# Placing the early raw inputs, the first weights and the v step of a fused attention, dense and expert kernel

## The chip, the cores and the metric

One core of a Trainium2 chip runs the whole kernel. The metric is the device time of one execution in microseconds; less is better. Runs of one kernel are given with their median.

## The reference, cut to what matters

```python
# q, k, v: (4, 8, 576, 64) float32; w_in (512, 2048), w_out (2048, 512) arrive as float64
scores = scale * (q @ k.T)                       # per batch and head
kth = np.partition(scores, -32, axis=-1)[..., -32:-31]
scores = np.where(scores >= kth, scores, -1e9)   # the 32 largest of each row stay
attn = softmax(scores)
x = (attn @ v)                                   # -> 2304 tokens of 512
x = softplus(x @ w_in) @ w_out                   # dense layer, hidden size 2048
e = argmax(x @ w_gate); g = softmax(x @ w_gate)[e]
out = g * (relu(x @ w1[e]) @ w2[e])              # one of 8 experts for each token
```

## The kernel before, in words

`part_one` does attention and the dense layer, `part_two` the experts. Two heads of one batch make a pair; batch 0 has pairs 0 to 3 in the list `pairs`, called the first to the fourth pair here (m = 0 to 3), and 16 loads of each of q, k and v are made in all. A pair is prepared once for its visits: q, k and v are loaded into tiles of 128 partitions by 576 float32 (`qn`, `kn`, `vn` from the pool `raw`, which has one buffer of each, RB = 1), their magnitudes are summed on ACT (`magnitudes`, line 338), and each is split into a half of 16 bits and the rest (lines 370 and 371 for k and q, 383 and 384 for v; the subtraction runs on DVE for the first pair and on POOL for the others). The halves of k are transposed by a DMA into `kt` (line 373), those of q by two DMAs into `q1` (line 376); two plain copies make `q2`, the same with its halves of partitions exchanged (lines 377 and 378). The halves of v are copied into `v16` by six DMAs (lines 388 to 390). `prep_split` does all this for the first four pairs, `prep_step` in three steps for all later ones. All these DMAs are issued on one queue, SP's, which works in order.

Attention runs over groups of two score tiles of 128 by 576. Each pair has two groups in the first sweep over batch 0, so the first pair belongs to groups 0 and 1, the second to 2 and 3, the third to 4 and 5, the fourth to 6 and 7. `emit_scores` makes a group's scores on PE (line 456, results `sa` and `sb`; a score needs q1, q2 and kt), `emit_softmax` finds the 32nd largest score on DVE (lines 496 to 522) and makes the masked exponents on ACT and POOL (lines 530 to 542), and a DMA transposes them (line 544). Three groups later (LAG = 3) `emit_av` multiplies them with v (line 559).

The weights of the dense layer come as float64 and are decoded in 32 chunks of 128 by 512: `decode` loads a chunk (line 238), and ACT, DVE and POOL build float32 from its words (lines 247 to 253); for w_in ACT and POOL then split it (lines 258 to 260). The list `dec_q` holds four chunks of w_in, then rows 0 to 3 of w_out, four of w_in, rows 4 to 7, and so on. `decode_some(2)` takes two of them ahead of the first group, and four more are emitted with each group (DECR = 4). The decoded w_out, `w_out_s`, is one tile of 16 rows (KF) of 512 float32 for each partition; its row f is first read by the second product of the dense layer (line 686).

When the tiles of a unit (two tiles of 128 tokens, in most) are complete, `moe_step` runs the dense layer on it, 16 steps of line 646 (x @ w_in) and line 686, and `route` then writes its rows and its places in `table`, which `clear_table` has filled beforehand. The first unit is complete after group 7, the second after the next sweep.

The order on each engine's queue and on SP's is set when the kernel is built, by a planner that runs a timeline with its own costs: of what is ready it takes what has the highest priority. Priority is the place in the program, moved forward by the offset of `tc.high_priority` (A_PREP = 150, AHEAD = 100). `tc.issue_after(x)` puts what is traced in its block behind x on x's queue.

## Time and profile before

| what | value |
| --- | --- |
| median of 3 runs | 1064.67 us (1059.51, 1064.67, 1066.27) |
| the profiled execution | 1059.72 us |
| its span in the trace | 1058.0 us |
| mean granted clock of TensorE | 0.936 of full speed |
| DMA | 156.97 MB, mean 148 GB/s |

The span is the time from the first to the last instruction that the trace shows; the profiled execution's own time is 1.72 us longer. In the rows below PE is TensorE, PEld its weight loads, DVE VectorE, ACT ScalarE, POOL GpSimd and SP the engine that issues DMAs (SPq is its queue). A time in brackets is how long the engine stood idle before the instruction, with what ended the wait. "x4" counts instructions that were merged into a row.

### The profile page before, as it was taken

To read this page: it belongs to the slowest core of one execution; us is meant where nothing else is said; L and a number is where in the kernel's file an instruction comes from. 1 tells how busy PE (TensorE), PEld (TensorE's weight loads), DVE (VectorE), ACT (ScalarE), POOL (GpSimd) and SP (SyncE) were. 2 spreads that over 40 slices of the span, in tenths; PEclk is the share of its full clock that TensorE was granted. 3 is DMA by queue.
4 is the path that set the end of the run, shared out by engine and by line. 5 is a ranking of instruction groups with operands and counts; after the bars stand their busy time and mean duration, and the time that the engine had idled before them with its cause. 6 is when DMAs were issued, how large, how long until landed. Compare 5 with 4: busy or idle time off the path is not lost.

```text
span 1058.0 us, 22206 instructions
## 1 busy us (share of the span) xinstructions
PE 885.0 (84%) x7146; PEld 655.0 (62%) x7146; DVE 849.3 (80%) x3021; ACT 801.2 (76%) x1866; POOL 604.0 (57%) x631
## 2 busy tenths in 40 slices
PE   1124359774998989998999999999999999999994
PEld 0013236443675656675666666676787989999993
DVE  4779999998997968996989999955356987777773
ACT  5878898988888979987998888863678555555552
POOL 3888898998767768876778777652001022111111
PEclk9986559876999989998999999999999999999998
DMA  7897799788799987669978855464301667666650
GB/s 188 193 205 189 180 192 193 179 168 172 114 131 164 138 152 129 117 80 150 152 131 120 99 90 95 72 86 131 102 12 31 170 220 243 242 212 230 237 202 23
DMA packets 295859, 156.97 MB, mean 148 GB/s; under 512 B 257524, under 2 KB 257652, under 8 KB 295732
## 3 DMA queue, kind: packets, MB, share of 16 engines
q1 hardware_dynamic: 292116, 145.73, 67.1%
q0 software_dynamic: 3616, 9.72, 2.6%
q8 instruction: 58, 0.95, 0.4%
q14 instruction: 69, 0.57, 0.2%
HBM read 77.89 MB, written 11.11 MB: 84 GB/s over the span
## 4 chain that ended last, share of the span: by engine, by line
PE 47%; DVE 13%; DMA 12%; ACT 9%; POOL 8%; issue 6%; SPq 4%; POOLq 0%; ACTq 0%; DVEq 0%
PE h L646 11%; PE h L996 9%; PE y L686 8%; PE y L1009 8%; PE y L683 3%; DVE mx L522 3%; DVE wk L518 3%; DMA xT<-xh 3%; POOL e L531 2%; POOL p L542 2%; DMA w<-in_moe_w_in_dram 2%; PE sb L456 2%; PE m L559 1%; ACT e L532 1%; PE sa L456 1%
## 5 line engine op out<-in xcount | busy, mean ns | idle before, releaser
L646 PE MATMUL h<-xT,w_in_s 128*128 128x256 f16 (+1 forms) x1920 | 228.7, 269 | 22.9 <-ACT sa L660 14.4
L686 PE MATMUL y<-w_out_s,g 128*128 128x512 f32 x480 | 229.0, 601 | 1.3 <-ACT g L661 1.2
L646 PEld LDWEIGHTS <-w_in_s 128*128 128x128 f16 x1920 | 174.9, 101 | 82.7 <-issue 52.7
L531 POOL TENSOR_TENSOR e<-s,e 128x576 f32<-128x576 f32 x144 | 204.0, 1432 | 17.7 <-ACT e L530 10.4
L522 DVE MAX8 mx<-wk 128x8 f32<-128x128 f32 (+2 forms) x432 | 200.9, 503 | 0.1
L542 POOL TENSOR_TENSOR p<-e,p 128x512 f16<-128x512 f32 x144 | 167.8, 1165 | 0.0
L456 PEld LDWEIGHTS <-q 128*128 128x128 f16 (+1 forms) x640 | 55.8, 108 | 175.4 <-issue 125.8
L518 DVE MATCH_REPLACE8 wk<-mx,wk 128x128 f32<-128x128 f32 (+1 forms) x432 | 145.1, 343 | 0.1
L686 PEld LDWEIGHTS y<-w_out_s,g 128*128 128x128 f32 x480 | 82.7, 192 | 64.0 <-issue 58.1
L976 POOL DMA_INDIRECT out_dram<-ot,idx x19 | 19.5, 1028 | 176.1 <-DVE ot L975 173.4
L532 ACT ACTIVATE e<-e,bias 128x576 f32<-128x576 f32 x144 | 110.4, 768 | 12.7 <-POOL e L531 12.2
L996 PEld LDWEIGHTS h<-xT,wf 128*128 128x128 f32 x864 | 111.8, 191 | 5.4 <-ACT wf L957 0.2
L996 PE MATMUL h<-xT,wf 128*128 128x256 f32 x864 | 113.9, 283 | 0.0
L456 PE MATMUL sa<-kt,q 128*128 128x256 f16 (+1 forms) x320 | 54.0, 302 | 71.0 <-DMA kt<-st 23.4
L1009 PE MATMUL y<-wf,hT 128*128 128x512 f32 x432 | 112.8, 398 | 0.0
L456 PE MATMUL sb<-kt,q 128*128 128x320 f16 (+1 forms) x320 | 62.7, 338 | 53.6 <-ACT s L502 53.5
L530 ACT ACTIVATE e<-s,kths 128x576 f32<-128x576 f32 x144 | 104.9, 767 | 0.8
L559 PEld LDWEIGHTS <-pT 128*128 128x128 f16 (+1 forms) x1440 | 86.8, 106 | 22.9 <-issue 19.8
L559 PE MATMUL m<-v,pT 128*128 128x65 f16 (+1 forms) x1440 | 93.9, 201 | 7.2 <-DVE xtail L586 4.3
L540 ACT ACTIVATE p<-e 128x576 f16<-128x576 f32 x144 | 97.4, 678 | 0.7
L541 POOL TENSOR_TENSOR p<-e,p 128x64 f16<-128x64 f32 x144 | 46.1, 320 | 70.4 <-ACT p L540 65.9
L1009 PEld LDWEIGHTS y<-wf,hT 128*128 128x128 f32 x432 | 76.7, 189 | 13.0
(235 smaller groups left out, 1791.1 us busy)
## 6 DMA issues: line engine op xcount, KB each, us to landing
w1r<-in_moe_w_dram SPq DMA_DIRECT2D x20, 1024.0 KB, 6.3
w2r<-in_moe_w_dram SPq DMA_DIRECT2D x20, 1024.0 KB, 7.8
w<-in_moe_w_in_dram SPq DMA_DIRECT2D x16, 512.0 KB, 4.0
w<-in_moe_w_out_dram SPq DMA_DIRECT2D x16, 512.0 KB, 4.0
rows<-xr SPq DMA_DIRECT2D x37, 128.2 KB, 3.1
qn<-in_q_dram SPq DMA_DIRECT2D x16, 288.0 KB, 4.1
kn<-in_k_dram SPq DMA_DIRECT2D x16, 288.0 KB, 6.1
vn<-in_v_dram SPq DMA_DIRECT2D x16, 288.0 KB, 3.5
```

Of the source, the lines that this page charges most:

```text
L456: last_qk[0] = nc.tensor.matmul(ps[p0:p1], lhsT=qs[:, h, r0:r1, :].rearrange("p r d -> p (r d)"), rhs=kt[:, k0:k1, cs], start=first, stop= ...
L518: nc.vector.match_replace(out=to, in_to_replace=mx[:, i, 8 * j:8 * j + 8], in_values=src[i], imm_value=NEG)
L522: nc.vector.max(out=mx[:, i, 8 * j + 8:8 * j + 16], in_=src[i])
L530: nc.scalar.activation(e[i], s[i], AF.Relu, bias=kths[:, 2 * gi + i], scale=-K_UP)
L531: nc.gpsimd.tensor_tensor(out=e[i], in0=s[i], in1=e[i], op=ALU.subtract)
L532: nc.scalar.activation(e[i], e[i], AF.Exp, bias=bt[:, i], scale=SCORE)
L542: nc.gpsimd.tensor_tensor(out=p16[:, S + D:], in0=e[i][:, 0:S - D], in1=p16[:, 0:S - D], op=ALU.subtract)
L559: nc.tensor.matmul(o[:, h, 0:D + 1], lhsT=pT(r), rhs=v16[:, h, c, 0:D + 1], start=r == 0, stop=r == R - 1)
L646: nc.tensor.matmul(hps[:, :n], lhsT=w_in_s[:, c, j, p, o:o + 128], rhs=xT[:, 0:len(u.tiles), r, c, :], start=m == 0, stop=m == 3 * KD - 1)
L686: nc.tensor.matmul(u.y[i], lhsT=g[:, cs], rhs=w_out_s[:, f, :], start=f == 0, stop=f == KF - 1)
L996: nc.tensor.matmul(h, lhsT=w1f[:, a, c, :], rhs=xT[:, b, c, :], start=n == 0, stop=n == 3 * KD - 1)
L1009: nc.tensor.matmul(y[i], lhsT=hT[g][:, a, i * 128:i * 128 + 128], rhs=w2f[:, b, :], start=g == 0 and n == 0, stop=g == KF2 - 1 and n == 2)
```

## The change

- The second pair's raw q, k and v are loaded into rows 12 to 15 of `w_out_s`, the third pair's into rows 8 to 11 (`ROOM`), which no weight has been written to yet. The second pair's loads are issued right behind the first's; the third's and the fourth's (which stays in `raw`) behind the first pair's last q transpose; the fifth's after the fourth is split.
- The halves of the second pair (k, q and v) lie in rows 4 to 7 of `w_out_s` (`STROOM`) instead of the pools `stg` and `row`.
- The v step of the first four pairs becomes a function, `prep_v`, that is traced at offset 20 (`A_V`) instead of 150; the first pair's magnitudes go with it.
- The first two weight chunks are traced at offset 150, behind the first pair's last q transpose.
- The fill of `table` is traced after them; its source lies in the last 146 columns of row 15 of `w_out_s`, no longer in a pool of its own.

Nothing of what is computed changes. The second pass that the kernel holds for inputs outside its bounds (`flags is None`) keeps the old loads. The diff:

```diff
@@ -48,6 +48,10 @@
 KVB = 4
 SWEEPS = [((0, 1), (8, 2, 3))] * 3 + [((0, 1), (8, 2), (3,))]
 UNITS = [[(b,2*i),(b,2*i+1)] for b in range(3) for i in range(2)]+[[(0,'tail0')],[(3,0),(3,1)],[(3,2),(1,'tail1')],[(3,3)]]
+ROOM = {1: 12, 2: 8}
+STROOM = 4
+V_NOW = 0
+A_V = 20
 XB = 1
 FLB = 4
 RB = 1
@@ -122,12 +126,6 @@
     table = dram.tile([E * NT + SLOT, 1], I32, name="table")
     rows = dram.tile([NT + 1, ROWW], F32, name="rows")
 
-    def clear_table():
-        with tc.tile_pool(name="fill", bufs=1) as p:
-            fill = p.tile([128, (E * NT + SLOT) // 128], I32, name="fill")
-            nc.gpsimd.iota(fill, pattern=[[0, (E * NT + SLOT) // 128]], base=TRASH, channel_multiplier=0)
-            nc.sync.dma_start(table.rearrange("(p a) o -> p (a o)", p=128), fill)
-
     zrow = const.tile([27, 19], F32, name="zrow")
     nc.vector.memset(zrow, 0.0)
     nc.sync.dma_start(rows[TRASH:TRASH + 1, :].rearrange("o (p a) -> (o p) a", a=19), zrow)
@@ -176,7 +174,6 @@
 
     def run(halves):
         nc.vector.memset(done, 0.0)
-        clear_table()
         with ExitStack() as p:
             late = part_one(tc, p, q, k, v, w_in, w_out, const, ident, before, ones, iota_e, reg_e, wg, ids,
                             ohcum, done, early, table, rows, flags if halves else None, sums, w_sums, e_sums, kths)
@@ -279,6 +276,11 @@
         nc.vector.tensor_scalar(bb, pb[:, 0:n], 1e-30, None, op0=ALU.max)
         return bb
 
+    def clear_table():
+        fill = w_out_s[:, KF - 1, DM - (E * NT + SLOT) // 128:].bitcast(I32)
+        nc.gpsimd.iota(fill, pattern=[[0, (E * NT + SLOT) // 128]], base=TRASH, channel_multiplier=0)
+        nc.sync.dma_start(table.rearrange("(p a) o -> p (a o)", p=128), fill)
+
     w_inv = wp.tile([128, DFF // C], F32, name="w_inv")
 
     def split_w_in(j):
@@ -313,27 +315,31 @@
                 f(*a)
 
 
-    pair = {}
+    pair, raws, last_t, last_l = {}, {}, {}, [None]
     v_up = wp.tile([128, B], F32, name="v_up")
     nc.vector.memset(v_up, 3.0e38)
 
     def load(m, i):
         b, hp = pairs[m]
-        t = raw.tile([128, R * D], F32, name="qkv"[i] + "n")
-        nc.sync.dma_start(t, (q, k, v)[i][b, 2 * hp:2 * hp + 2].rearrange("h (p r) d -> (h p) (r d)", r=R))
+        if flags is not None and m in ROOM:
+            a = ROOM[m] * DM + i * R * D
+            t = w_out_s.rearrange("p k c -> p (k c)")[:, a:a + R * D]
+        else:
+            t = raw.tile([128, R * D], F32, name="qkv"[i] + "n")
+        last_l[0] = nc.sync.dma_start(t, (q, k, v)[i][b, 2 * hp:2 * hp + 2].rearrange("h (p r) d -> (h p) (r d)", r=R))
         pair[m][0][i] = t
 
     def prep_load(m):
         src = [None] * 3
         bd = sm.tile([128, 3], F32, name="bd") if flags is None else sums[:, m]
-        pair[m] = (src, bd)
+        pair[m] = raws[m] = (src, bd)
         for i in range(3):
             load(m, i)
         if flags is None:
             magnitudes(m, stg.tile([128, R * D], F16, name="st"))
 
     def magnitudes(m, junk):
-        src, bd = pair[m]
+        src, bd = raws[m]
         for i, t in enumerate(src):
             nc.scalar.activation(junk, t, AF.Abs, accum_out=bd[:, i:i + 1])
 
@@ -353,6 +359,20 @@
             nc.scalar.activation(src[i], src[i], AF.Copy, scale=sc[:, i:i + 1])
         pair[m] = (*src, sc)
 
+    def staging(m, i):
+        cols = 2 * D + 2 if i == 2 else 2 * D
+        if flags is not None and m == 1:
+            a = STROOM * DM * 2 + i * R * 2 * D
+            st = w_out_s.rearrange("p k c -> p (k c)").bitcast(F16)[:, a:a + R * cols]
+            st = st.rearrange("p (r c) -> p r c", c=cols)
+        elif i == 2:
+            st = stg.tile([128, R, cols], F16, name="vs")
+        elif i and m < ST0:
+            st = row.tile([128, R, 2, D], F16, name="p16", bufs=PB if flags is not None else 2)
+        else:
+            st = stg.tile([128, R, 2, D], F16, name="st")
+        return st if i == 2 or len(st.shape) == 4 else st.rearrange("p r (s d) -> p r s d", d=D)
+
     def prep_split(m):
         qn, kn, vn, sc = pair[m] if flags is None else (*pair[m][0], None)
         sub = nc.vector if m < DVS else nc.gpsimd
@@ -363,22 +383,26 @@
             magnitudes(m, q2[:, 0].rearrange("p r d -> p (r d)"))
         for i, xs in enumerate((kn, qn)):
             xv = xs.rearrange("p (r d) -> p r d", d=D)
-            if i and m < ST0:
-                st = row.tile([128, R, 2, D], F16, name="p16", bufs=PB if flags is not None else 2)
-            else:
-                st = stg.tile([128, R, 2, D], F16, name="st")
+            st = staging(m, i)
             nc.scalar.activation(st[:, :, 0, :], xv, AF.Copy)
             sub.tensor_tensor(out=st[:, :, 1, :], in0=xv, in1=st[:, :, 0, :], op=ALU.subtract)
             if i == 0:
                 nc.sync.dma_start_transpose(out=kt, in_=st.rearrange("p r s d -> p (r s d)"))
             else:
                 for h in range(2):
-                    nc.sync.dma_start_transpose(out=q1[:, h], in_=st[64 * h:64 * h + 64].rearrange("p r s d -> p (r s d)"))
+                    last_t[m] = nc.sync.dma_start_transpose(
+                        out=q1[:, h], in_=st[64 * h:64 * h + 64].rearrange("p r s d -> p (r s d)"))
         nc.sync.dma_start(q2[0:64], q1[64:128])
         nc.sync.dma_start(q2[64:128], q1[0:64])
-
+        pair[m] = q1, q2, kt, vn, sc
+        if V_NOW:
+            prep_v(m)
+
+    def prep_v(m):
+        q1, q2, kt, vn, sc = pair[m]
+        sub = nc.vector if m < DVS else nc.gpsimd
         v16 = kv.tile([128, 2, 5, 2 * D + 2], F16, name="v16")
-        vs = stg.tile([128, R, 2 * D + 2], F16, name="vs")
+        vs = staging(m, 2)
         xv = vn.rearrange("p (r d) -> p r d", d=D)
         nc.scalar.activation(vs[:, :, 0:D], xv, AF.Copy)
         sub.tensor_tensor(out=vs[:, :, D + 2:], in0=xv, in1=vs[:, :, 0:D], op=ALU.subtract)
@@ -847,9 +871,12 @@
     credit, started = 0, 0
     for i in range(-1, n + LAG):
         if i == -1:
-            with tc.high_priority(offset=AHEAD):
-                for m in range(RB):
-                    prep_load(m)
+            with tc.high_priority(offset=2 * A_PREP):
+                for m in range(RB if flags is None else 2):
+                    with ExitStack() as loads_in_order:
+                        if m:
+                            loads_in_order.enter_context(tc.issue_after(last_l[0].ins))
+                        prep_load(m)
                 prep_scale(0)
         for m, step in steps.get(i, []):
             with tc.high_priority(offset=A_PREP):
@@ -859,8 +886,20 @@
                 if to_scale:
                     prep_scale(to_scale.pop()[0])
                 prep_split(done_prep)
-                if done_prep + RB < len(pairs):
-                    prep_load(done_prep + RB)
+                if flags is None:
+                    if done_prep + RB < len(pairs):
+                        prep_load(done_prep + RB)
+                elif done_prep in (0, 3):
+                    if done_prep:
+                        prep_load(4)
+                    else:
+                        with tc.issue_after(last_t[0].ins):
+                            prep_load(2)
+                            prep_load(3)
+            if not V_NOW:
+                with tc.high_priority(offset=A_V):
+                    prep_v(done_prep)
+            with tc.high_priority(offset=A_PREP):
                 if done_prep + 1 < len(pairs):
                     to_scale.append((done_prep + 1, i + SCALE))
             done_prep += 1
@@ -868,7 +907,10 @@
             with tc.high_priority(offset=AHEAD):
                 prep_scale(to_scale.pop()[0])
         if i == -1:
-            decode_some(2)
+            with tc.high_priority(offset=A_PREP), ExitStack() as behind_q:
+                behind_q.enter_context(tc.issue_after(last_t[0].ins))
+                decode_some(2)
+            clear_table()
         if i + 1 < n:
             with tc.high_priority(offset=A_SC):
                 emit_scores(i + 1)
```

## Rows read from the trace of the kernel before

**Rows 1.** page of the kernel before, busy time of each engine

```profile
PE 885.0 (84%) x7146; PEld 655.0 (62%) x7146; DVE 849.3 (80%) x3021; ACT 801.2 (76%) x1866; POOL 604.0 (57%) x631
```

**Rows 2.** table by stage of all engines (windows, us from the span's start)

```profile
core 0: us, PE busy (x) PEld busy (x) DVE busy (x) ACT busy (x) POOL busy (x), PEclk, DMA share, GB/s
0.00:20.00 20.00, 3.14 (x12) 1.64 (x13) 6.74 (x18) 11.99 (x25) 7.90 (x19) 1.00 0.81 183
20.00:150.00 130.00, 40.08 (x373) 26.26 (x373) 113.62 (x380) 107.36 (x215) 108.54 (x107) 0.76 0.86 194
150.00:265.00 115.00, 84.49 (x698) 54.27 (x698) 107.35 (x350) 104.90 (x239) 106.21 (x104) 0.81 0.82 176
265.00:705.00 440.00, 420.82 (x3765) 285.63 (x3764) 392.95 (x1633) 378.17 (x923) 330.90 (x353) 0.98 0.78 119
705.00:1058.00 353.00, 336.44 (x2307) 287.22 (x2303) 228.61 (x644) 198.76 (x469) 50.45 (x52) 0.99 0.50 157
```

**Rows 3.** timeline of SP's queue: start, length, line, transfer

```profile
3.61 0.93 SPq L238 DMA_DIRECT2D w<-in_moe_w_in_dram  x2
...
7.43 1.34 SPq L376 DMA_TRANSPOSE q<-p  x1
...
10.79 1.28 SPq L376 DMA_TRANSPOSE q<-p  x1
...
17.93 0.62 SPq L389 DMA_DIRECT2D v<-vs  x1
...
21.30 0.53 SPq L323 DMA_DIRECT2D qn<-in_q_dram  x1
21.88 0.42 SPq L323 DMA_DIRECT2D kn<-in_k_dram  x1
...
22.87 0.85 SPq L238 DMA_DIRECT2D w<-in_moe_w_in_dram  x2
```

**Rows 4.** waits of SP's queue, 0 to 12 us: total, times, longest

```profile
SPq L376 <- DMA table<-fill: 1.9, 1, 1.9
```

**Rows 5.** timeline of PE; idle time before, and its releaser, in brackets

```profile
17.30 0.80 PE L456 MATMUL sa<-kt,q 128*128 128x256 f16 x3 [3.30 <-DMA q<-q]
...
33.59 1.01 PE L456 MATMUL sa<-kt,q 128*128 128x256 f16 x4 [10.09 <-DMA kt<-st]
...
57.20 0.40 PE L456 MATMUL sa<-kt,q 128*128 128x256 f16 x1 [12.58 <-DMA q<-st]
...
62.98 0.26 PE L559 MATMUL m<-v,pT 128*128 128x65 f16 x1
```

**Rows 6.** timeline of DVE, same columns

```profile
30.55 0.70 DVE L249 TENSOR_SCALAR y<-y 128x512 uint32<-128x512 uint32 x1 [1.97 <-ACT y L247]
...
32.27 0.70 DVE L249 TENSOR_SCALAR y<-y 128x512 uint32<-128x512 uint32 x1 [0.63 <-ACT y L247]
...
57.26 0.70 DVE L249 TENSOR_SCALAR y<-y 128x512 uint32<-128x512 uint32 x1 [1.67 <-ACT y L247]
...
63.30 0.43 DVE L496 TENSOR_TENSOR sb<-sb,s 128x256 f32<-128x256 f32 x1 [1.48 <-PE sb L456]
```

**Rows 7.** chain that ended last, in order of time: start, us, what

```profile
14.61 2.56 DMA q<-q
...
23.35 8.25 DMA w<-in_moe_w_in_dram
...
264.77 3.98 PE h L646 x22
```

**Rows 8.** groups of ACT, 9 to 19 us: busy, mean ns, idle before

```profile
L251 ACT ACTIVATE w<-w 128x512 int32<-128x512 uint32 x2 | 1.3, 638 | 0.0
L258 ACT ACTIVATE w_in_s<-t 128x512 f16<-128x512 f32 x2 | 1.3, 630 | 2.5 <-POOL t L253 2.5
L247 ACT ACTIVATE y<-w 128x512 f32<-128x512 f32 x2 | 1.2, 624 | 2.0 <-DMA w<-in_moe_w_in_dram 2.0
L259 ACT ACTIVATE w_in_s<-t 128x512 f16<-128x512 f32 x2 | 1.2, 612 | 0.0
```

## The prediction

> **What bounds the kernel now.** I read the busy times first [rows 1]: PE is busy for 84% of the span, DVE for 80%, ACT for 76%. No engine is full over the whole, so the next view is the table by stage [rows 2], in which the reader is to look for the engine that is nearly full in each stage. From 265 us to 705 PE is busy for 420.82 of 440 us (95.6%) and after 705 for 336.44 of 353 (95.3%), at a granted clock of 0.98 and 0.99, which is the 2.4 GHz level. There only TensorE work counts. Before 265 PE is idle for long stretches, and the three elementwise engines carry the stage: from 150 to 265 DVE is busy for 107.35 of 115 us (93.3%), ACT for 104.90, POOL for 106.21. From 20 to 150 they hold less: DVE 113.62 of 130 (87.4%), ACT 107.36, POOL 108.54. In the first 20 us DVE has 6.74.
>
> So the start feeds a chain. The second unit of the dense layer starts on PE at 264.77 [rows 7] and PE runs nearly full from there; what comes before it is a fixed amount of softmax, weight decoding and input preparation on DVE, ACT and POOL. The change touches the start alone. What it is worth is how much earlier that fixed amount is done, and a microsecond saved there should come out nearly whole at the end, since the stage behind is PE's.
>
> The third view is the queues at the start. PE waits three times for inputs of a pair [rows 5]: until 17.30 for the doubled copies of the first pair's q, 10.09 us until 33.59 for kt of the second, 12.58 us until 57.20 for q of the third. PE being idle costs nothing here by itself; what counts is where DVE runs dry with it. DVE stands 1.97 and 0.63 us ahead of 30.55 and 32.27, the time of the second pair, and 1.67 and 1.48 ahead of 57.26 and 63.30, the time of the third [rows 6]. The cause is on SP [rows 3]: one buffer for each raw input, and one queue in order. kn and vn of the second pair go out at 21.88 and after, behind the transposes and the v copies of the first; the qn at 21.30 is already the third pair's.
>
> **The table.** The write of `table` goes ahead of the first transpose now, and SP's first transpose waits 1.9 us for it [rows 4]. With the write behind the transposes that wait is gone, and the last q transpose of the first pair, at 10.79 [rows 3], could go at 8.9. What is late next for that transpose is DVE's subtraction of the first q, which the wait has outlasted. Its bounds are -1.9 (all passes to the first scores) and 0 (another transfer takes its place in the wait). The new place of the fill, the last columns of w_out's last row, adds a wait to the last w_out decode; it has over 100 us of room, so I cost it at nothing.
>
> **The loads of pairs two to four.** No byte is added. The second pair's three loads go out right behind the first's, so its kt no longer waits for a free buffer and for 21.88. Its halves get a place of their own and wait for no staging buffer. The third pair's loads go behind the first pair's last q transpose. What is removed is DVE's idle time: 1.97 + 0.63 = 2.6 us for the second pair, 1.67 + 1.48 = 3.15 for the third, 5.75 together [rows 6]. The fourth pair's loads still go into the one raw buffer, behind the last reader of the first pair's v, and I count nothing for them. Bounds for the sum of this part: 0, if the gaps only move to another wait (the decoder's ACT step is the releaser of three of the four, and it waits for the weight's DMA), and 8.3, if the whole stage from 20 to 150 rises to the fill of the stage behind it: 113.62 / 0.933 = 121.7 instead of 130 [rows 2]. I take 5.75, which rests on named gaps. It is hidden if DVE stays dry for the weights; then the whole 5.75 is lost.
>
> New waits: the w_out rows lent out are decoded late in the list (rows 4 to 7 from the thirteenth chunk, 8 to 11 from the twenty-first, 12 to 15 from the twenty-ninth, of 32). The POOL add that writes row 4 now waits for the second pair's v copies to leave their place; behind it on POOL stand the softmax subtractions, and ACT's exponents wait for those. Two chunks are emitted ahead of the first group and four with each group after it, so the thirteenth belongs to the third group, whose scores start at 33.59 now [rows 5]; the second pair's v copies, though late, should be out by then. I cost it at nothing; if it holds POOL once, that is one v copy set, six issues of 0.62 us, 3.7 us [rows 3].
>
> **v at low priority.** The same operations, later: per pair one ACT step, one subtraction, one memset and six SP issues of 0.62 us, 3.7 us of SP [rows 3], move from between the transposes to where SP has room. The three magnitudes of the first pair move with it. The first product with v runs at 62.98 [rows 5], so the first pair's v has 40 us of room. I cost it at nothing on either side; SP's gain is the cover for the loads above.
>
> **The first weights.** The two chunks that now go out at 3.61 go behind the last q transpose, with priority. Now their ACT steps, 1.3 + 1.3 + 1.2 + 1.2 = 5.0 us [rows 8], lie in time in which ACT has nothing else to do: it is busy for 11.99 of the first 20 us [rows 2]. The second pair's preparation takes that place. This is a swap, costed at nothing if the sum of work is all that counts, and at 5.0 if ACT is the engine that is late after 20 us.
>
> **Transfers ahead of the doubled copies.** This is the term with two signs. Behind the last q transpose SP may now issue qn, kn, vn of the third pair and two weights, while the copies that double q wait for the transposes to land. The trace has that very group: five such transfers from 21.30 on, the last of which lands at 23.35 + 8.25 = 31.60 [rows 3, 7], 10.3 us after the first was issued. Now the copies land at 14.61 + 2.56 = 17.17 [rows 7]. With the five ahead of them from 8.9 + 1.3 = 10.2 on, they would land at 20.5, 3.3 us later than now; with nothing ahead, 1.9 earlier than now, at 15.3. I take the middle, 0.7 later, because the copies themselves are short and the weights behind them may well be issued after them.
>
> The Trainium skill, DMA: Bandwidth & Descriptors, section Queues, rings and completion order, says that each DMA engine consumes the descriptors of a queue in ring order. By that rule the late end, 20.5, would hold whenever the five are issued first, and this part of the change would speak against itself; the trace agrees so far as the 8.25 us of the last weight goes.
>
> **Sum.** -5.75 for the two pairs, +0.7 for the first scores, nothing for the rest: -5.0 us. The profiled execution took 1059.72 us, which makes 1054.7 by it; the median of the three runs is 1064.67, 4.9 us higher, and I give the forecast against that: 1059.7.
>
> **Rivals.** First, a full recovery: the stage from 20 to 150 us gains its 8.3 and the table's 1.9 comes through, 10.2 us, 1054.5. For it speaks that POOL and ACT are also under 84% full there, against it that DMA is already at 0.86 in that stage [rows 2]; earlier loads don't make it emptier.
>
> Second, no change, 1062 to 1067: the order on every queue is set at build time by a planner with its own costs, so the second pair's transposes may still stand behind other things, or the gaps reappear as waits for weights, which ended most of them. Here the change does not do what it says.
>
> Third, slower: the five transfers go ahead of the doubled copies (+3.3), and the weights' 5.0 us of ACT come out of the full stage (together +8.3). They arrive with the backlog, so both hang on that one group in SP's queue. It decides if the copies are issued behind the five: then even the recovered 5.75 leaves +2.6, and with none recovered it is +8.3. The middle is 1070.1. For it speaks the group at 21.30, against it that DVE has two pairs' scores to work on once the first copies land.
>
> **How the numbers follow.** I give the forecast (gain of 3 to 8 us) 0.44, the full recovery 0.24, no change 0.17, slower 0.15. The predicted time is 1059.7. Under 1054.5 or so would take the full recovery and a little more. One per cent, 10.6 us, is about what a measurement of this kernel can tell from no change. Most of the full recovery's chance lies at that line, so faster by over 1% gets 0.23; slower by over 1% takes the far end of the third rival and whatever the planner's reordering does further on, 0.11; the rest is 0.66. The range reaches from 1047, past the full recovery by the 4.9 us that lie between the profiled run and the median, and some more, to 1071, the middle of the third rival and a little more.
>
> **What would show it.** In the changed profile: the second pair's kn issued before 5 us; the first transpose near 5.5 to 6 instead of 7.43; PE's wait for the second pair's kt and the third pair's q gone or under 3 us; DVE from 20 to 150 at 90% or more; the second unit's first product near 260 instead of 264.77; the stage of PE behind it as long as now. The slower case shows as the doubled copies issued behind the third pair's loads and landing after 19 us. The prediction is wrong if the gaps are gone and 264.77 has not moved, or if it has moved and the end has not: then the stage behind is not PE's alone.

## The result and the profile after

The changed kernel takes 1069.7 us (median of 13 runs, 1066.39 to 1073.53) against 1061.44 us for the kernel before, run beside it (13 runs, 1056.81 to 1066.27): a ratio of 1.0078, 95% interval 1.0058 to 1.0097. The forecast was 1059.7. The profiled execution has a span of 1065.7 us, 7.7 more than before.

The busy time of each engine, on the page of the kernel after, has hardly moved against [rows 1]; no work was added:

```profile
PE 888.5 (83%) x7146; PEld 658.7 (62%) x7146; DVE 847.8 (80%) x3021; ACT 802.3 (75%) x1866; POOL 602.5 (57%) x631
```

So the 7.7 us are a matter of when work is done. The table by stage of the kernel after, with the stages and columns of [rows 2]:

```profile
0.00:20.00 20.00, 2.29 (x9) 1.13 (x10) 4.42 (x14) 12.22 (x26) 7.29 (x20) 1.00 0.96 215
20.00:150.00 130.00, 45.37 (x389) 29.78 (x389) 112.54 (x388) 103.96 (x206) 106.95 (x107) 0.82 0.83 184
150.00:265.00 115.00, 87.57 (x685) 56.26 (x683) 103.76 (x329) 104.86 (x244) 103.86 (x101) 0.81 0.80 180
265.00:705.00 440.00, 409.44 (x3725) 279.25 (x3723) 394.20 (x1637) 377.06 (x914) 327.37 (x349) 0.99 0.76 118
705.00:1066.00 361.00, 343.82 (x2347) 292.24 (x2344) 232.89 (x658) 204.22 (x479) 57.01 (x58) 0.98 0.51 155
```

Two things are to be seen. By 265 us DVE has done 4.42 + 112.54 + 103.76 = 220.72 us of work against 227.71 before: it is 7.0 us behind. The softmax is what is behind: the last weight chunk is decoded before 265 us in both, and DVE has begun 23 groups by then (line 520) against 24 before (line 496). And from 265 to 705 PE is idle for 30.6 of 440 us where it was idle for 19.2. The granted clock there is 0.99 against 0.98, so the clock isn't the cause of that idle time.

SP's queue after (columns of [rows 3]):

```profile
2.68 0.43 SPq L329 DMA_DIRECT2D w_out_s<-in_k_dram  x1
...
5.32 1.33 SPq L393 DMA_TRANSPOSE q<-p  x1
...
9.18 1.27 SPq L393 DMA_TRANSPOSE q<-p  x1
10.50 0.58 SPq L235 DMA_DIRECT2D w<-in_moe_w_in_dram  x1
...
12.57 0.58 SPq L395 DMA_DIRECT2D q<-q  x1
13.21 1.29 SPq L393 DMA_TRANSPOSE q<-w_out_s  x1
14.55 0.59 SPq L396 DMA_DIRECT2D q<-q  x1
15.18 0.59 SPq L329 DMA_DIRECT2D w_out_s<-in_q_dram  x1
...
23.29 0.66 SPq L412 DMA_DIRECT2D v<-vs  x1
...
46.00 0.37 SPq L235 DMA_DIRECT2D w<-in_moe_w_in_dram  x1
...
61.83 0.53 SPq L235 DMA_DIRECT2D w<-in_moe_w_in_dram  x1
```

The second pair's kn goes out at 2.68, the first transpose at 5.32, the last q transpose of the first pair at 9.18: the start does what was asked of it. But v copies, which began before 20 us [rows 3], now begin at 23.29, and the third and fourth weight, issued together at 22.87 before [rows 3], go out at 46.00 and 61.83.

DVE's timeline after, columns of [rows 6]:

```profile
15.29 0.70 DVE L246 TENSOR_SCALAR y<-y 128x512 uint32<-128x512 uint32 x1 [7.08 <-ACT y L244]
...
19.93 0.43 DVE L520 TENSOR_TENSOR sb<-sb,s 128x256 f32<-128x256 f32 x1 [3.21 <-ACT s L490]
...
67.36 0.70 DVE L246 TENSOR_SCALAR y<-y 128x512 uint32<-128x512 uint32 x1 [3.22 <-ACT y L244]
...
76.27 0.42 DVE L520 TENSOR_TENSOR sb<-sb,s 128x256 f32<-128x256 f32 x1
```

ACT's timeline after, same columns:

```profile
14.64 0.62 ACT L244 ACTIVATE y<-w 128x512 f32<-128x512 f32 x1 [4.35 <-DMA w<-in_moe_w_in_dram]
...
64.75 0.68 ACT L407 ACTIVATE vs<-vn 128x576 f16<-128x576 f32 x1 [4.26 <-DMA v<-vs]
```

The first group reaches DVE at 19.93, the seventh at 76.27. Before, their rows on DVE's timeline were

```profile
19.01 0.43 DVE L496 TENSOR_TENSOR sb<-sb,s 128x256 f32<-128x256 f32 x1 [6.20 <-PE sb L456]
...
84.77 0.43 DVE L496 TENSOR_TENSOR sb<-sb,s 128x256 f32<-128x256 f32 x1 [1.14 <-PE sb L456]
```

so the seventh group is 8.5 us ahead. In exchange ACT stands for 4.26 us, because the one staging buffer `vs` still holds the third pair's halves whose copies are queued on SP, and DVE stands for 3.22 behind it.

Behind 75 us the gain is lost: up to there DVE has been busy for 50.86 us against 50.29 before, from 75 to 150 us for 66.10 against 70.07. ACT's waits for weights from 75 to 150 us in the kernel before (total, times, longest):

```profile
ACT y L247 <- DMA w<-in_moe_w_out_dram: 2.0, 3, 1.6
...
ACT y L247 <- DMA w<-in_moe_w_in_dram: 1.2, 1, 1.2
...
ACT xr L247 <- DMA w<-in_moe_w_in_dram: 0.6, 2, 0.3
```

The same waits after:

```profile
ACT y L244 <- DMA w<-in_moe_w_out_dram: 5.0, 5, 2.2
ACT y L244 <- DMA w<-in_moe_w_in_dram: 4.5, 3, 3.1
ACT xr L244 <- DMA w<-in_moe_w_in_dram: 1.9, 1, 1.9
```

That is 3.8 us before and 11.4 after. The last weight chunk ends on POOL at 232.28 before and at 251.53 after (the last decoding of `w_out_s` on POOL's timeline). Before:

```profile
230.98 1.30 POOL L253 TENSOR_TENSOR w_out_s<-xr,w 128x512 int32<-128x512 int32 x1
```

After:

```profile
250.24 1.29 POOL L250 TENSOR_TENSOR w_out_s<-xr,w 128x512 int32<-128x512 int32 x1 [1.24 <-ACT p L564]
```

Still, the second unit starts on PE 4.4 us earlier than the 264.77 of [rows 7]; PE's timeline after:

```profile
260.41 2.79 PE L670 MATMUL h<-xT,w_in_s 128*128 128x256 f16 x24 [1.45 <-DMA xT<-xh]
```

and then PE waits more. Its longest waits from 265 to 705 before:

```profile
PE h L646 <- ACT sa L660: 13.8, 6, 5.0
PE sb L456 <- ACT s L502: 2.2, 4, 1.1
```

And after:

```profile
PE y L710 <- ACT g L685: 7.2, 5, 2.5
PE h L670 <- ACT sa L684: 7.0, 3, 3.2
PE sa L480 <- ACT s L490: 5.7, 5, 3.4
PE h L670 <- DMA xT<-xh: 5.5, 2, 3.4
```

The new ones are waits for ACT (`g`, `s`) and for attention rows (`xh`), and the softmax that is left over from before 265 goes through the same engines; that the one causes the other is how I read it, and no run tests it by itself.

### The profile page after: what moved, and what is told of

Its sections match the earlier page's. It is cut to its first block, busy times and chain, and to the rows that moved or that the text cites. A ratio compares the mean times of both kernels' runs of the same rounds, so it can differ in the third digit from the quotient of the medians.

```text
span 1065.7 us, 22211 instructions
## 1 busy us (share of the span) xinstructions
PE 888.5 (83%) x7146; PEld 658.7 (62%) x7146; DVE 847.8 (80%) x3021; ACT 802.3 (75%) x1866; POOL 602.5 (57%) x631
## 4 chain that ended last, share of the span: by engine, by line
PE 40%; DVE 15%; DMA 13%; ACT 13%; POOL 9%; issue 5%; SPq 4%; POOLq 0%; ACTq 0%; DVEq 0%
PE h L1038 9%; PE y L1051 8%; PE h L670 8%; PE y L710 6%; PE y L707 3%; DVE mx L546 3%; POOL e L555 3%; DVE wk L542 3%; POOL p L566 3%; DMA pT<-p 2%; DMA xT<-xh 2%; DMA w<-in_moe_w_out_dram 2%; ACT p L564 2%; ACT e L556 2%; ACT e L554 2%
## 5 line engine op out<-in xcount | busy, mean ns | idle before, releaser
L670 PE MATMUL h<-xT,w_in_s 128*128 128x256 f16 (+1 forms) x1920 | 227.3, 268 | 24.0 <-ACT sa L684 10.2
L555 POOL TENSOR_TENSOR e<-s,e 128x576 f32<-128x576 f32 x144 | 203.5, 1431 | 11.4 <-ACT e L554 5.8
```

The lines of the kernel that those rows point to most:

```text
L555: nc.gpsimd.tensor_tensor(out=e[i], in0=s[i], in1=e[i], op=ALU.subtract)
L670: nc.tensor.matmul(hps[:, :n], lhsT=w_in_s[:, c, j, p, o:o + 128], rhs=xT[:, 0:len(u.tiles), r, c, :], start=m == 0, stop=m == 3 * KD - 1)
```

## The experiments

The question was first which part costs the time, then by what way. The theories: that the late decoding of the weights is the price (D where a letter is used), that the held staging buffer `vs` is (G), that work lost to idle time at the start is (A), and that the order of later work scatters by as much (B). Other letters are explained where they stand. Edits are to the changed kernel, or to the kernel before where that is said; "..." marks lines of an edit that are not shown. Each ratio is to runs of the kernel before on the same chip. The table gives for each run the ratio, the end of the last weight chunk on POOL, ACT's waits for weights from 75 to 150 us, and DVE's busy time by 265 us, all read as above. The last three columns come from one profiled execution of each.

| run | v | ratio (95%) | last chunk | ACT waits | DVE by 265 |
| --- | --- | --- | --- | --- | --- |
| before | at once | 1 | 232.3 | 3.8 | 227.7 |
| after | late | 1.0078 (1.0058 to 1.0097) | 251.5 | 11.4 | 220.7 |
| a1_v_now | at once | 0.9987 (0.9957 to 1.0017) | 231.5 | 3.8 | 229.8 |
| b3_v_low | late | 1.0064 (1.004 to 1.0088) | 243.2 | 7.4 | 224.8 |
| a4_loads_alone | at once | 1.0034 (1.0006 to 1.0063) | 235.2 | 7.1 | 221.4 |
| b1_weights_later | at once | 1.0061 (1.003 to 1.0092) | 240.9 | 13.0 | 220.7 |
| x2_weights_early | late | 1.0194 (1.0138 to 1.025) | 269.8 | 6.9 | 222.3 |
| x3_weights_early_v_now | at once | 1.0023 (0.9995 to 1.005) | 247.5 | 8.6 | 225.1 |
| b4_weights_put_off | at once | 1.0257 (1.0223 to 1.029) | 276.5 | 5.7 | 220.2 |
| d1_decode_ahead | late | 0.9994 (0.9967 to 1.0021) | 224.1 | 10.2 | 224.2 |
| a5_vs_third_apart | late | 1.0016 (0.9991 to 1.004) | 258.8 | 8.1 | 221.6 |
| a7_vs_apart_decode_ahead | late | 1.0005 (0.998 to 1.003) | 234.6 | 12.2 | 227.9 |
| a6_v_copies_on_pool | late | 1.01 (1.0075 to 1.0125) | 254.3 | 9.5 | 218.6 |
| d2_v_now_decode_ahead | at once | 0.9891 (0.9857 to 0.9926) | 225.4 | 3.7 | 230.4 |
| b6_before_decode_ahead | at once | 1.0021 (0.9988 to 1.0055) | 236.7 | 5.4 | 223.6 |
| p4_d2_av60 | at once | 0.996 (0.9944 to 0.9975) | 226.3 | 3.7 | 230.2 |
| p2_after_lag | late | 1.0064 (1.0038 to 1.0091) | 257.2 | 10.8 | 222.1 |
| p1_before_lag | at once | 1.0015 (0.9997 to 1.0034) | 240.4 | 3.8 | 222.5 |

**Which part.** a1_v_now: v at once again, all else as changed.

```diff
-V_NOW = 0
+V_NOW = 1
```

> The changed kernel with the v step of the four pairs back at offset 150. Theory A (work lost at the start: idle time that the elementwise engines cannot make up): ACT's 4.26 us in front of v at 64.75 and DVE's 3.22 at 67.36 go, the ratio to the kernel before falls from 1.008 to about 1.005 (1066 us). Theory B (the order of the later stages, set anew by the planner, cost the time, and the start does not matter): 1069.7 within 2 us or anything else within 6, with no relation to the idle time before 150 us.

Measured 0.9987: the loss is gone, where theory A expected some of it to stay (1.005). ACT's waits for weights are back at 3.8 us, although the third and fourth weight go out at 30.76, 8 us later than before:

```profile
ACT y L244 <- DMA w<-in_moe_w_out_dram: 2.4, 3, 0.9
...
ACT xr L244 <- DMA w<-in_moe_w_in_dram: 1.0, 2, 0.8
...
ACT y L244 <- DMA w<-in_moe_w_in_dram: 0.4, 1, 0.4
```

b3_v_low: the other way round, v alone at low priority in the kernel before (with `prep_v` split off as in the change).

```diff
...
+            with tc.high_priority(offset=20):
+                prep_v(done_prep)
...
```

> The kernel before with one part alone: v of the four pairs traced at offset 20. Theory D (v's copies, put off on SP, come between the weights' loads, the weights get late, and that is the price): the third weight load goes from 22.9 us to over 30, the last chunk from 232 us to 240 or later, ratio 1.003 to 1.010. Theory E (v at low priority is harmless by itself, it needs the early loads of the other pairs with it): ratio 1.000 within 0.003, last chunk within 5 us of 232.

Measured 1.0064. The two together name v: it costs by itself, and taking it out of the change takes the loss out. On SP's timeline the third and fourth weight go out at 25.91 and 44.58 in it:

```profile
25.91 0.53 SPq L238 DMA_DIRECT2D w<-in_moe_w_in_dram  x1
44.58 0.38 SPq L238 DMA_DIRECT2D w<-in_moe_w_in_dram  x1
```

a4_loads_alone: only the loads and the second pair's halves in new places; v, first weights and table as before.

```diff
-V_NOW = 0
+V_NOW = 1
...
-            with tc.high_priority(offset=A_PREP), ExitStack() as behind_q:
-                behind_q.enter_context(tc.issue_after(last_t[0].ins))
-                decode_some(2)
-            clear_table()
+            decode_some(2)
...
```

> Only the loads and halves in their new places stay of the change: v at offset 150, the first weights at offset 0, the table at the start in its own pool. Theory D: groups 2 to 6 up to 5 us earlier, the third weight load at some 30 to 34 us, so the last chunk 0 to 15 us later and the ratio 0.998 to 1.004. What the prediction counted for this part, 5.75 us, would be 0.9946.

Measured 1.0034: the loads alone bring nothing. They also cost something in this form: the first pair's last q transpose goes out at 14.24 instead of 10.79, and the first group reaches DVE at 22.48 instead of 19.01, so this is no clean measure of the 5.75 us. b1_weights_later: the first two chunks alone moved, in the kernel before.

```diff
...
-            decode_some(2)
+            with tc.high_priority(offset=A_PREP), ExitStack() as behind_q:
+                behind_q.enter_context(tc.issue_after(last_t[0].ins))
+                decode_some(2)
```

> The kernel before with the first two weight chunks behind the first pair's last q transpose, alone. Theory D: only the first two chunks are some 5 us late, the third load still goes out near 23 to 27 us, the last chunk within 6 us of 232, ratio 0.998 to 1.004. If the idle time in front of the first weights is a price by itself (5.0 us of ACT): 1.004 to 1.007.

Measured 1.0061. The later first weights leave ACT and POOL idle at the start, as the row of this run's table by stage shows against 11.99 us of ACT and 7.90 of POOL in [rows 2]; in a1_v_now, where the second pair's inputs are there to fill the time, ACT is at 11.86. But that idle time is not shown to be the price: by 150 us DVE has done 120.57 us of work here against 120.36 before, and the 7.0 us that it lacks at 265 are lost after that. A loss of 0.6% is also within what a later order moves (end of this section).

```profile
0.00:20.00 20.00, 3.13 (x12) 1.64 (x13) 5.47 (x16) 8.99 (x18) 4.35 (x16) 1.00 0.85 184
```

**By what way.** x2_weights_early and x3_weights_early_v_now: the first two chunks right behind the first pair's loads, without and with v at once.

```diff
...
-            with tc.high_priority(offset=A_PREP), ExitStack() as behind_q:
-                behind_q.enter_context(tc.issue_after(last_t[0].ins))
+            with tc.high_priority(offset=6 * A_PREP), ExitStack() as behind_v:
+                behind_v.enter_context(tc.issue_after(first_l[0].ins))
                 decode_some(2)
```

> The changed kernel with the first two weight chunks right behind the first pair's loads, as in the kernel before, and the second pair's loads behind them. Theory A: DVE's 7.08 us before its first weight step at 15.29 shrink to about 2.5, the decoding is some 10 us less late, and the ratio falls from 1.008 to about 1.004 (1065.5 us). Theory B: no relation, 1069.7 within 6.

> Both of the other two edits: the loads' new places and the later table alone stay of the change. Theory A: both losses go, ratio 0.996 to 1.001 (about 1060 us), and the busy time of DVE up to 265 us is at least the 227.7 of the kernel before. Theory B: no relation, 1069.7 within 6.

Measured 1.0194 and 1.0023. The first is a plain miss: the first two weights are there early, issued at 2.21, and the kernel became slower still; its third weight goes out at 65.57 us, its last chunk ends at 269.8. With v at once most of that loss is gone, but 1.0023 and DVE's 225.1 us miss the 0.996 to 1.001 and the 227.7 that were expected too. b4_weights_put_off, in the kernel before, delays the weights, with no other edit.

```diff
...
+                if i == 1:
+                    put_off.enter_context(tc.issue_after(last_t[2].ins))
+                decode_some(0 if i == 0 else 2 * DECR if i == 1 else DECR)
```

> The kernel before with the weights from the third chunk on held behind the third pair's q transposes (two of the first group's time and more), nothing else changed. Theory D: as late as in the run with early first weights and v low (third load at some 66 us, last chunk 37 us late), so ratio 1.012 to 1.022. Theory F (lateness of the weights is only a sign, the work is the same and engines fill up with groups in its place): ratio 1.000 to 1.005.

Measured 1.0257, over the 1.012 to 1.022 expected, with the last chunk at 276.5. So late weights cost by themselves when they are that late. Two edits were then meant to mend one consequence each. d1_decode_ahead puts each group's chunks ahead of v:

```diff
-            with tc.high_priority(offset=0):
+            with tc.high_priority(offset=60):
                 decode_some(DECR)
```

> The changed kernel with the four weight chunks of each group at offset 60 instead of 0, so that they are no longer put off. Theory A, pure form (the total of work done by 265 us counts, not which): the last chunk lands 10 to 20 us earlier than 251.5, the early groups later, and the ratio stays at 1.008 within 0.003. A third theory, C (the weights being 20 us late is itself the price, since groups 20 to 23 share DVE with them): ratio near 1.002.

a5_vs_third_apart gives the third pair's halves of v a place in rows 12 to 15 of `w_out_s`, which the second pair's raw inputs have left:

```diff
+        elif i == 2 and flags is not None and m == 2:
+            a = ROOM[1] * DM * 2
+            st = w_out_s.rearrange("p k c -> p (k c)").bitcast(F16)[:, a:a + R * cols]
+            st = st.rearrange("p (r c) -> p r c", c=cols)
```

> The changed kernel, with the third pair's halves of v in the second pair's used raw rows instead of the one buffer vs, so that ACT's step for the fourth pair's v need not wait for the third's late copies. Theory G (that held buffer, 4.26 us of ACT and 3.22 of DVE at 65 to 67 us, is the price of v at low priority): ratio 1.002 to 1.005. Theory D (the late weights are): the third weight load stands still later on SP here than in the changed kernel, so the ratio is 1.008 to 1.015, although the stall is gone.

Measured 0.9994 and 1.0016. The first is far from theory A's 1.008 and a little under C's 1.002, the second a little under G's range and outside D's. Each takes off most of the loss, though a5_vs_third_apart leaves the weights later than in the changed kernel (the third goes out at 62.17, the last chunk ends at 258.8). And d1_decode_ahead mends both: ACT no longer stands in front of v there, and its last chunk ends before that of the kernel before, on POOL's timeline:

```profile
222.81 1.30 POOL L250 TENSOR_TENSOR w_out_s<-xr,w 128x512 int32<-128x512 int32 x1 [0.93 <-DVE rc L609]
```

a6_v_copies_on_pool issues the v copies on GpSimd's queue, to take them off SP.

```diff
+        vq = nc.gpsimd if flags is not None else nc.sync
...
-            nc.sync.dma_start(v16[0:64, h], src[:, 0:R:2])
...
+            vq.dma_start(v16[0:64, h], src[:, 0:R:2])
...
```

> The changed kernel, v still at offset 20, but the first four pairs' 24 v copies are issued on GpSimd's queue instead of SP's. Theory D: SP is free for the weights, the third load goes from 46.0 us to under 35, and the ratio falls from 1.008 to 0.997 to 1.003 (less if 24 issues of about 1 us hold GpSimd). Theory F: 1.008 stays.

Measured 1.01, a miss for theory D: the third weight goes out at 26.61 instead of 46.00 and the fourth at 38.12 instead of 61.83, and the kernel is no faster. But the copies now keep POOL busy, which decodes and splits too, and DVE is busy for 39.51 us from 20 to 75 us against 46.44 in the changed kernel; so it tells nothing certain about SP. Its first stage in the table by stage:

```profile
0.00:20.00 20.00, 2.61 (x11) 1.47 (x12) 5.10 (x14) 10.96 (x22) 12.73 (x29) 1.00 0.99 224
```

One of the issues on POOL's timeline:

```profile
9.41 0.91 POOL L413 DMA_DIRECT2D v<-vs  x1
```

**Two prices or one, and where the gain is.** a7_vs_apart_decode_ahead has both mends, v still late.

> The changed kernel with v still at low priority, but the third pair's v halves in a place of their own (the 4.26 us stall of ACT goes, as the run with that edit alone showed) and each group's weight chunks at offset 60 (the lateness of the last chunk goes, as the run with that edit alone showed). If the held staging buffer and the late weights are two prices of v at low priority, both are mended and it comes out near 0.994 of the kernel before, better than either edit alone (1.0016 and 0.9994). If they are one price, mending the second adds nothing: 0.999 to 1.002.

Measured 1.0005: mending the second adds nothing. It hardly could, as d1_decode_ahead has lost ACT's stall already; so this run does not tell one price from two. d2_v_now_decode_ahead has v at once and the chunks ahead (the edits of a1_v_now and d1_decode_ahead), b6_before_decode_ahead only the chunks ahead, in the kernel before.

> The changed kernel with both mends: v at offset 150 and each group's weights at offset 60. Theory D: the last chunk lands earlier than 232 us, ratio 0.993 to 0.999, below the kernel before; if the order of the early groups and the weights is a mere swap once the weights are not late, 0.998 to 1.002.

> The kernel before with nothing changed but each group's weight chunks at offset 60 instead of 0. If the gain of the changed kernel with v at once and the chunks ahead (0.989) is that of the chunks' place alone, this gives the same: 0.988 to 0.993. If that gain is the earlier inputs of the pairs, which the late weights only hid, this stays at 0.998 to 1.003.

Measured 0.9891 and 1.0021. The first beats both kernels, by more than was expected: 1053.49 us (1051.69 to 1055.72, 4 runs). The chunks' place alone isn't it. DVE in d2_v_now_decode_ahead by 265 us, row of its table by stage:

```profile
0.00:265.00 265.00, 137.34 (x1131) 89.41 (x1131) 230.37 (x746) 226.59 (x487) 222.92 (x231) 0.80 0.84 187
```

The last three change only the order of later work, from the first product with v on (62.98 in [rows 5]): A_AV = 60 instead of 150, in the kernel before, in the changed one and in d2_v_now_decode_ahead.

```diff
-A_AV = 150
+A_AV = 60
```

> A control: the kernel before with the offset of the products with v (A_AV) at 60 instead of 150; the start's queues stay as they are, the order changes from about 150 us on. It shows how far a new order of the later stages alone moves the time. Theory B (the later order rules) 0.99 or 1.01; theory D: 1.000 within 0.004.

> The changed kernel with only the products with v at 60 steps of priority instead of 150; the start stays as it is. If the loss of 0.8% belongs to the start (weights late, buffer held), it stays at 1.004 to 1.011. If it is the scatter of later orders, it can come out anywhere from 0.996 to 1.004.

> The changed kernel with v at once and the weight chunks ahead (0.989 of before), and the products with v put at 60 steps of priority instead of 150, which changes only the order of later work. If 0.989 is owed to the start, it stays within 0.985 to 0.994. If it was luck of the later order, it goes back to 0.997 or more.

Measured 1.0015, 1.0064 and 0.996. The loss of the changed kernel stays; the gain of d2_v_now_decode_ahead shrinks by 0.7% but not to nothing, between the two ranges that were expected. Held against p1_before_lag, which has the same later order, the changed kernel loses 1.0064 / 1.0015, 0.5%, and d2_v_now_decode_ahead gains 0.996 / 1.0015, 0.5%. So a difference of up to 0.7% between two kernels of this table can be the later order alone, and only what shows in several pairs is taken as shown.

## Why the prediction was wrong

**The step that failed** is the one on v: "The same operations, later [...] move from between the transposes to where SP has room [...] I cost it at nothing on either side". In four pairs of kernels that differ in v's place alone, each measured against the kernel before, late v is dearer: 1.0064 (b3_v_low to before), 1.0078 / 0.9987 = 1.009 (after to a1_v_now), 0.9994 / 0.9891 = 1.010 (d1_decode_ahead to d2_v_now_decode_ahead), 1.0194 / 1.0023 = 1.017 (x2_weights_early to x3_weights_early_v_now). That is 7 to 18 us of 1061, where the forecast had 0. The forecast's error is 1.0078 against 0.9953 (1059.7 / 1064.67), 1.25%; 0.9 points of it are v's, by a1_v_now. The reason given, 40 us of room until the first product with v [rows 5], was true and not what counted. It left out whom the 24 copies keep waiting when they go out late: on SP the weights, which are traced at offset 0, behind them; and ACT, which needs `vs`, the one buffer that they hold.

**Which of the two it is** the runs settle only in part. Mending the buffer takes 0.6% off the changed kernel, mending the weights' place 0.8%, both together 0.7%: these are not two sums that add up, and the second of these edits takes ACT's stall away as well. Late weights alone do not carry all of it, since a5_vs_third_apart has them later still than the changed kernel and is at 1.0016. And with both mended late v still costs 1.0005 / 0.9891 = 1.2% against d2_v_now_decode_ahead, which has v at once and the chunks ahead (of which up to 0.7% may be later order, as p4_d2_av60 shows). What the eight kernels with v late have in common in the trace is ACT waiting for weights from 75 to 150 us, 6.9 to 12.2 us, where a1_v_now, d2_v_now_decode_ahead, p4_d2_av60, p1_before_lag and the kernel before have 3.7 or 3.8. In d1_decode_ahead:

```profile
ACT y L244 <- DMA w<-in_moe_w_in_dram: 3.1, 2, 2.2
...
ACT y L244 <- DMA w<-in_moe_w_out_dram: 2.8, 1, 2.8
...
ACT xr L244 <- DMA w<-in_moe_w_in_dram: 2.2, 1, 2.2
...
ACT xr L244 <- DMA w<-in_moe_w_out_dram: 2.1, 1, 2.1
```

In the changed kernel these 11.4 - 3.8 = 7.6 us, DVE's 7.0 us behind at 265 and the 7.7 us at the end are of one size. But that is no more than a mark, and the carrier is not shown. The other five kernels with v at once wait 5.4 to 13.0 us, the longest of all in b1_weights_later; a7_vs_apart_decode_ahead waits 12.2 us and is level with the kernel before, x2_weights_early 6.9 and loses 1.9%. Why ACT still waits when the chunks are issued earlier stays open too.

**The stage behind.** "A microsecond saved there should come out nearly whole at the end, since the stage behind is PE's" failed too, in the way that the prediction named: 264.77 moved to 260.41, about the 260 forecast, and the end went the other way. The 95.6% busy PE of [rows 2] is fed by softmax groups on ACT and DVE, of which the changed kernel has one more still to begin at 265; as I read it, that comes back as PE's waits. DVE's busy time by 265 tells the end better than the start of the second unit does: of the kernels with 227.7 us or more (before, a1_v_now, a7_vs_apart_decode_ahead, d2_v_now_decode_ahead, p4_d2_av60) none is over 1.0005. Below that they lie from 0.9994 to 1.0257, and p1_before_lag lacks 5.2 us at 265 and is at 1.0015, so it does not rank them finely.

**The loads.** The gaps of the second and third pair were recovered in part: PE no longer waits for kt of the second and the transposed q of the third (for the second pair's doubled copies it waits 4.84 us, until 26.86), and DVE is busy for 46.44 us from 20 to 75 against 43.55 before, 2.9 of the 5.75 counted. The sign "DVE from 20 to 150 at 90% or more" was not met, with 112.54 of 130 us, 86.6%. Nor is it shown that the new loads closed the gaps. Rows from 20 to 75 us, columns of [rows 2], of the kernel before, the changed one, a1_v_now and b3_v_low:

```profile
20.00:75.00 55.00, 11.90 (x92) 6.95 (x91) 43.55 (x148) 42.14 (x87) 40.56 (x42) 0.98 0.86 195
20.00:75.00 55.00, 16.82 (x115) 10.30 (x115) 46.44 (x165) 43.13 (x88) 41.29 (x42) 1.00 0.85 185
20.00:75.00 55.00, 14.04 (x95) 8.16 (x94) 45.96 (x152) 43.79 (x90) 40.52 (x42) 0.87 0.92 204
20.00:75.00 55.00, 15.60 (x110) 9.60 (x109) 46.62 (x165) 43.56 (x89) 41.81 (x43) 0.85 0.92 203
```

Late v alone, with the old loads, brings DVE to 46.62 us there and leaves PE 2.3 us of wait for kt and none for the transposed q, and that kernel is 0.6% slower: work done early at the start is not yet a gain at the end. Of the kernels with the new loads, v at once and the chunks at their old priority, a4_loads_alone is at 1.0034, with its own delay at the start, x3_weights_early_v_now at 1.0023, and a1_v_now at 0.9987 (0.9957 to 1.0017) where about 0.995 was due. The gain appears with the chunks ahead (0.9891, and 0.996 under another later order). So the change with v at once and the chunks ahead is worth 4 to 12 us. Why it takes the chunks ahead is not shown, since a1_v_now has ACT's waits and the last chunk at the level of the kernel before already.

**The table** went as said: the first transpose at 5.32 instead of 7.43, the last q transpose at 9.18 where 8.9 was forecast. **The first weights**: ACT is busy for 12.22 of the first 20 us against 11.99, the swap on ACT. DVE pays for it with 4.42 against 6.74, since its step waits 7.08 us for them; a cost of 2.3 us that the term left out; by 75 us the changed kernel (50.86) and a1_v_now (51.08) have made it good against 50.29 before. **The doubled copies**: the last of them is issued at 14.55, ahead of the third pair's loads at 15.18, and the first scores reach DVE at 19.93, 0.9 us later than before (19.01), with +0.7 forecast. The size was about right, but by luck. Of the five transfers that were feared only one weight (10.50) went out ahead. What took the table's gain back was a transpose of the second pair's q between the two copies, at 13.21, so that the second copy went out when it did before (14.61 in [rows 7]); the sum did not have it. **The new wait on POOL** for row 4 of w_out did not show among POOL's waits from 20 to 150 us.

**The rivals.** The slower one named 1070.1, and 1069.7 was measured, but not by its mechanism: of the five transfers only one went ahead of the doubled copies. For the same reason the rule of the Trainium skill (DMA: Bandwidth & Descriptors, section Queues, rings and completion order) that was weighed there was hardly put to the test: one weight stood ahead of those copies, and the second of them reached PE at 17.83, 3.3 us after its issue, where it took 2.7 before (14.61 to 17.30 in [rows 5, 7]). No change, as second rival, had the reappearance of the gaps "as waits for weights", which is nearest to what was seen (11.4 us against 3.8); what it lacked is that these can come out larger than before. The sum missed a wait because v was looked at only from its own reader's side.

## What to carry to other kernels

Work that is moved to a low priority may have no reader that minds, but it has a queue and a buffer: ask what stands behind it on the queue, at a priority lower still, and who waits for the buffer it holds until then. Before a gap is booked as gain, ask what the engine that is fed next needs, and if that comes from the same queue; here late v alone closed the gaps and the kernel got slower, and the earlier inputs paid only with v in its old place and the weights ahead. Two edits of one start, v's old place and the chunks ahead, each without a gain alone, gave 0.4 to 1.1% together (the lower end is within what a later order moves), so parts are to be tried with and without each other, and a control that only reorders later work tells how much of a difference is to be believed.

## What was not expected of the hardware

A DMA issued from GpSimd's queue counts as work of that engine: the v copies took 0.56 to 0.91 us of POOL each, about as long as one issue takes on SP's queue in the changed kernel (0.59 to 0.66). Six issues stand between two subtractions there, and POOL was busy for 12.73 of the first 20 us instead of 7.29 in the changed kernel. That kernel is 1% slower than the kernel before; how much of this is POOL's no run shows.
